# Gated attention and FFN mix on one core: the second FFN product summed in three blocks a token tile instead of one

## The chip, the cores and the metric

The kernel runs on 1 core of one Trainium2 chip. The metric is device time in microseconds; three runs of the kernel before took 1418.3, 1418.87 and 1421.13 us, median 1418.87 us. All other numbers of the time before come from one execution that was profiled.

## What is computed

Two branches over the same 2048 tokens of width 512, mixed by a gate for each token. Branch A is softmax attention with 32 heads of 16; branch B is a gated FFN of width 1792. Everything is fp32; the kernel splits each fp32 operand of its dense products into a high and a low part and adds three products (high by high, high by low, low by high).

```python
x = A_x
g = sigmoid((x * gate_w).sum(-1, keepdims=True))
a = softmax(q @ k.T * 16 ** -0.5) @ v @ wo      # per head; q, k, v = x @ wqkv
b = (silu(x @ w1) * (x @ w3)) @ w2
out = g * a + (1 - g) * b
```

## The kernel before

After a preparation of some 95 us the program is one long list of TensorE work that is written out by hand. The string `order` (lines 734 to 738) has a letter for each piece of TensorE work, and the loop at line 743 walks it:

- Q: one unit of scores, 128 keys by 512 queries for two heads (`score`, line 713). Its two matmuls go to two halves of the array's rows and of a two-bank PSUM tile `S`, of which there are two. ScalarE takes the exponential of the unit (line 723) into a tile `p`.
- P: two units of `p` times V, into the bank `acc` (`pv`, line 702). With the last key tile, `evac` (line 685) copies `acc` out and sends it to DRAM.
- F: one step of the dense work, by `feed` (line 654).

A period of the first 83 (`one`) is 8 Q, 21 F and 4 P; a later one (`two`) is 8 Q, 15 F and 4 P. The last one has 6 Q, 12 F and 4 P. In all there are 2418 F in the string; what is left of the dense work then runs alone, in the loop at line 779. After it come, at full height of the array, the products of the output projection that need the last head (lines 784 to 820). They wait for a chain of transfers that begins with the last `evac`: row sums out to DRAM and back, a reciprocal, out and back again, a multiplication, a split into halves (lines 773 and 776 to 816).

A step F gives one matmul to each of two lanes: rows 0 to 63 of the array (upper) and rows 64 to 127 (lower). A block is one PSUM bank of output. The upper lane runs all its products of a block over the first 64 contraction rows, then the lower lane runs the same number over the other 64 rows into the same bank, while the upper lane is at the next block. Three rules of `feed` set the pace:

```python
used = st["started"] - 3
if st["upper"] is None and (used < 0 or used < st["ended"] and left_at[used] + rest <= clock):
...
if st["lower"] is None and ready and ready[0][0] + gap <= issued:
```

There are three banks, so the upper lane starts a block only if the block three earlier has ended, and 7 counts have gone by since (`rest`; Q and F are one count, P is four). The lower lane takes a block when 3 scores have been issued since the upper lane left it (`gap`). If a lane has nothing, the step holds one matmul, or none.

The blocks, in order (`blocks`, line 630): 136 of 12 products a lane (q and k projections, then the FFN's first half, line 409), 16 of 42 products (the FFN's second half, one for each tile of 128 tokens, `h_product`, line 514), and 6 of 12 (the output projection of token tiles 0 to 5, `o_product`, line 592). The 42 are 14 row tiles of w2 by three products. VectorE takes each finished bank out of PSUM: for the second half, `h_done` (line 529) multiplies it by 1 - g into a tile `gs` and sends that to the DRAM tensor `B_d`, from where it comes back for the final sum in `mix` (line 601).

When the lower lane has done a quarter of a tile's products, line 520 loads and splits the same quarter for the tile after next (`load_piece`, `halves_of`): a transfer by SP's queue into a staging tile `sg`, then two GpSimd operations. The loads of the next head pair's Q and K (`load_step`, line 269), the stores of `evac` and the fetches of `divide` (line 564) go through the same SP queue, in program order. The reciprocal of `divide` (line 555) stands in VectorE's order among the evictions and waits for a transfer.

Of the kernel before, what the change touches and what calls it, by code (L numbers as in the profile page):

```python
# [8 lines left out]
F32 = mybir.dt.float32  # L9
# [3 lines left out]
OP = mybir.AluOpType  # L13
# [11 lines left out]
NT = S // P  # L25
ND = D // P
NF = F // P
# [6 lines left out]
def gated_mix_kernel(ctx: ExitStack, tc: tile.TileContext, x, wqkv, wo, w1, w3, w2, gate_w, out):  # L34
# [18 lines left out]
    nc = tc.nc  # L53
# [27 lines left out]
    def slot(tag, dtype=F32R, shape=(P, 512)):  # L81

        return (fw if tag[0] == "f" else fk).tile(list(shape), dtype, name=tag, bufs=BUFS.get(tag, 2))
# [4 lines left out]
    def bank():  # L88
        return psum.tile([P, 512], F32, name="f", bufs=3)
# [13 lines left out]
    omg = const.tile([P, NT], F32, name="omg")  # L103
# [206 lines left out]
    def load_weights(chunk):  # L310
        out = []
        for n, w in zip("13", chunk["src"]):
            r = slot("fr", F32, (P, ND, P))
            nc.sync.dma_start(r, w.rearrange("(k p) n -> p k n", p=P))
            if chunk["first"]:
                wh = slot("raw", F32R, (P, ND, P))
                wl = slot("raw" if n == "1" else "gw", F32R, (P, ND, P))
            else:
                wh = slot("fh" + n, F32R, (P, ND, P))
                wl = slot("fl" + n, F32R, (P, ND, P))  # L320
            nc.gpsimd.tensor_copy(wh, r)  # L321
            nc.gpsimd.tensor_sub(wl, r, wh)
            out.append((wh, wl))
        chunk["w"] = out

    chunks = [dict(src=(wqkv[:, P * c:P * c + P], wqkv[:, D + P * c:D + P * c + P]), first=c == 1)
              for c in range(1, ND)]
# [77 lines left out]
    def w_product(chunk, which, b):  # L405
        def product(ps, r, n):
            w = chunk["w"][which]
            k, i = divmod(n, 3)
            nc.tensor.matmul(ps, w[i == 2][r, k, :], (xL if i == 1 else xH)[b][r, k, :],  # L409
                             start=n == 0 and r.start == 0, stop=n == 3 * ND - 1 and r.start > 0)  # L410
        return product
# [3 lines left out]
    def qk_done(c, i, b):  # L415
        def done(ps):
            nonlocal qk_left
            lo = slot("gs", F32)
            hi = slot("sg")
            nc.vector.tensor_copy(lo, ps)  # L420
            nc.gpsimd.tensor_copy(hi, lo)
            nc.gpsimd.tensor_sub(lo, lo, hi)
            store_qk(i, c, b, hi, lo)
            qk_left -= 1
        return done
# [71 lines left out]
    def load_piece(t, q):  # L497
        hi, lo = (slot(SETS[t % 2][2 * q + i]) for i in range(2))
        tag = "fr" if t == 0 or t == 1 and q < 2 else "sg"
        n = min(4, NF - 4 * q)  # L500
        src = h_d[512 * q:512 * q + P * n, P * t:P * t + P].rearrange("(f p) t -> p f t", p=P)
        halves_of(src, hi[:, 0:P * n], lo[:, 0:P * n], tag)
        hs.setdefault(t, []).append((hi, lo))

    def load_wo(k):
        if k < 2:
            hi, lo = w2H[3][:, 2 + k, :], w2L[3][:, 2 + k, :]
        else:
            both = wk.tile([P, 2, 512], F32R, name=f"p{NP - k + 1}")
            hi, lo = both[:, 0, :], both[:, 1, :]  # L510
        halves_of(wo[P * k:P * k + P, :], hi, lo, "sg")
        wo_[k] = hi, lo

    def h_product(t):
        def product(ps, r, n):
            f, i = divmod(n, 3)
            q, o = divmod(f, 4)
            nc.tensor.matmul(ps, hs[t][q][i == 2][r, P * o:P * o + P], (w2L if i == 1 else w2H)[q][r, o, :],  # L518
                             start=n == 0 and r.start == 0, stop=n == 3 * NF - 1 and r.start > 0)
            if r.start and i == 2 and (o == 3 or f == NF - 1):  # L520
                if t + 2 < NT:
                    load_piece(t + 2, q)
                elif t == NT - 2:
                    load_ot(q)
                elif q < 2:
                    load_ot(4 + q)
        return product

    def h_done(t):
        def done(ps):  # L530
            y = slot("gs", F32)
            nc.vector.tensor_scalar(y, ps, omg[:, t:t + 1], None, op0=OP.mult)  # L532
            nc.sync.dma_start(B_d[P * t:P * t + P, :], y)
            if t in (4, 5, 6):
                later.append(lambda: load_wo((0, 1, 3)[t - 4]))
            if t == NT - 1:
                stages.append(rest_of_o())
        return done


    def load_ot(t):
        n = (0, 1, 2, 3, 2, 3, 0, 1)[t]
        hi, lo = (slot(SETS[0][2 * n + i]) for i in range(2))
        halves_of(N_d[:, P * t:P * t + P].rearrange("(k p) t -> p k t", p=P), hi[:], lo[:], "fr" if t >= 4 else "sg")
        ot[t] = hi, lo
# [46 lines left out]
    def o_product(t):  # L592
        def product(ps, r, n):
            if n == 0 and r.start:
                load_bt(t)
            k, i = divmod(n, 3)
            nc.tensor.matmul(ps, ot[t][i == 2][r, P * k:P * k + P], wo_[k][i == 1][r, :],  # L597
                             start=n == 0 and r.start == 0, stop=n == 3 * ND - 1 and r.start > 0)
        return product
# [5 lines left out]
    def o_done(t):  # L605
        def done(ps):
            mix(t, ps)
            if t < 2:
                load_ot(t + 6)
            if t in (3, 4):  # L610
                load_bt(t + 3, "fh1" if t == 3 else "fh3")
        return done
# [10 lines left out]
    def rest_of_o():  # L623
        for k in range(ND - 1):
            for b in (2, 3):
                load_o(k, b)
                for _ in range(4):
                    yield

    def blocks():  # L630
        last = len(chunks) - 1
        turns = [(m, b) for m in range(last - 1) for b in range(NB)]
        turns += [(last - i, b) for two in ((0, 1), (2,), (3,)) for i in (1, 0) for b in two]
        for m, b in turns:
            for which in range(2):
                if m < ND - 1:
                    yield w_product(chunks[m], which, b), qk_done(m + 1, which, b), 3 * ND
                else:
                    yield w_product(chunks[m], which, b), (up_done if which else gate_done)(m - ND + 1, b), 3 * ND
                if (b, which) == (1, 0) and m < last - 1 or (m, b, which) == (last - 1, 0, 1):  # L640
                    load_weights(chunks[m + 1])
        for t in range(NT):
            yield h_product(t), h_done(t), 3 * NF
        for t in range(NT // 2 - 2):
            yield o_product(t), o_done(t), 3 * ND

    NBLOCK = 8 * len(chunks) + NT + NT // 2 - 2
    source = blocks()

    ready, state_f = [], dict(upper=None, lower=None, started=0, ended=0)  # L650
# [128 lines left out]
    while feed(0, 0):  # L779
        pass  # L780
    assert state_f["ended"] == NBLOCK and not small and not later and not stages and not soon and not loads


    for t in (NT // 2 - 2, NT // 2 - 1):
        ps = bank()
# [4 lines left out]
    for t in range(NT // 2, NT):  # L790
        n, r = divmod(t - NT // 2, 2)
# [6 lines left out]
        if r == 0:  # L798
            y = wk.tile([P, 2, 512], F32, name=f"p{free.pop(0)}")
# [12 lines left out]
    for b in (2, 3):  # L812
        o, r = orr[b - 2]
# [34 lines left out]
```

## Time and profile before

| what | number |
|---|---|
| median of three runs | 1418.87 us (1418.3 to 1421.13) |
| profiled execution | span 1417.6 us, 1.3 us under that median; the page gives no time of it beside the span |
| TensorE matmul, busy | 1408.8 us, 99% |
| ScalarE, busy | 1033.2 us, 73%, of which the exponentials 967.5 us |
| VectorE, busy | 449.4 us, 32% |
| GpSimd, busy | 321.1 us, 23% |

Rows of a timeline read: start in us, duration in us, engine, line, operation, output and inputs by the program's names, shapes, and how many alike were merged (x). A bracket gives the idle time of the engine before it and what ended it. Rows of a group give total busy time and the mean in ns of one. A matmul's duration is longer than its distance to the next one, since matmuls are pipelined: the pace is read from the starts. PEld is the loading of weights, which overlaps the matmuls, SPq the issuing of transfers by SP's queue.

### The profile page before, as it was taken

How to read it: one execution, taken by the hardware profiler on the slowest of the kernel's cores; microseconds unless marked ns; L12 is line 12 of the kernel's file. 1: busy time of each engine (PE TensorE's matmuls, PEld its weight loads, DVE VectorE, ACT ScalarE, POOL GpSimd, SP SyncE). 2: the span in 40 equal slices, each digit the busy share in tenths (PEclk: the TensorE clock that was granted, in tenths of full speed). 3: DMA queues.
4: the chain of work that ended last, by engine and by line, in shares of the span. 5: the costliest groups of instructions: out<-in, count | busy, mean ns of one | idle time of the engine just before them, and what ended most of it. 6: DMA issues, size and time to landing. Idle time of an engine off the chain costs nothing.

```text
span 1417.6 us, 28518 instructions
## 1 busy us (share of the span) xinstructions
PE 1408.8 (99%) x11399; PEld 833.7 (59%) x11399; DVE 449.4 (32%) x845; ACT 1033.2 (73%) x1153; POOL 321.1 (23%) x356
## 2 busy tenths in 40 slices
PE   9999999999999999999999999999999999999998
PEld 7865656656556566565565665655555555554556
DVE  4421102464555545455464545400000000000013
ACT  4556767777777777777777777777788778877870
POOL 5014443011011100110110015441332332233230
PEclk9999999999999999999999999999999999999999
DMA  7554455342124432223233234543534443345445
GB/s 197 141 121 114 126 140 128 73 110 69 46 61 85 113 69 61 70 72 87 68 76 79 76 81 122 136 101 74 126 81 102 104 105 70 66 112 106 106 133 182
DMA packets 112668, 141.42 MB, mean 100 GB/s; under 512 B 16400, under 2 KB 70672, under 8 KB 109456
## 3 DMA queue, kind: packets, MB, share of 16 engines
q1 hardware_dynamic: 110384, 135.72, 39.6%
q10 hardware_dynamic: 2144, 3.80, 0.8%
q8 instruction: 92, 1.51, 0.5%
q14 instruction: 48, 0.39, 0.1%
HBM read 90.70 MB, written 48.76 MB: 98 GB/s over the span
## 4 chain that ended last, share of the span: by engine, by line
PE 93%; POOL 0%; DMA 0%; DVE 0%; ACT 0%; issue 0%; SPq 0%; ACTq 0%; POOLq 0%
PE acc L706 32%; PE f L409 27%; PE S L719 19%; PE f L518 11%; PE f L597 1%; PE f L95 0%; PE f L97 0%; PE f L96 0%; DMA fr<-in_B_w_dram 0%; PE S L97 0%; PE S L96 0%; PE S L95 0%; POOL xL L489 0%; POOL fl L489 0%; DVE sg L458 0%; POOL xH L488 0%
## 5 line engine op out<-in xcount | busy, mean ns | idle before, releaser
L723 ACT ACTIVATE p<-S 128x1024 f32<-128x1024 f32 x1024 | 967.5, 1026 | 308.4 <-PE S L719 307.1
L706 PE MATMUL acc<-p,V 128*17 128x512 f32 x4096 | 473.5, 594 | 0.0
L719 PE MATMUL S<-Qt,Kt 50*128 50x512 f32 x2048 | 427.9, 413 | 1.1 <-POOLq L278 0.6
L719 PEld LDWEIGHTS S<-Qt,Kt 50*128 50x128 f32 x2048 | 193.8, 184 | 187.4 <-ACT p L723 80.4
L706 PEld LDWEIGHTS acc<-p,V 128*17 128x17 f32 x4096 | 102.8, 97 | 274.1 <-issue 273.9
L409 PE MATMUL f<-xL,fh 64*128 64x512 f32 x1024 | 205.1, 391 | 0.0
L409 PE MATMUL f<-xH,fl 64*128 64x512 f32 x1024 | 204.9, 390 | 0.0
L409 PE MATMUL f<-xH,fh 64*128 64x512 f32 x1024 | 204.7, 390 | 0.0
L440 DVE RECIPROCAL sg<-sg 128x64 f32<-128x64 f32 x448 | 201.2, 509 | 1.9
L409 PEld LDWEIGHTS f<-xL,fh 64*128 64x128 f32 x1024 | 99.4, 187 | 21.2
L409 PEld LDWEIGHTS f<-xH,fl 64*128 64x128 f32 x1024 | 98.5, 185 | 20.1
L409 PEld LDWEIGHTS f<-xH,fh 64*128 64x128 f32 x1024 | 99.4, 187 | 17.7
L321 POOL CAST fh<-fr 128x512 fp32r<-128x512 f32 x32 | 21.6, 674 | 371.1 <-DMA fr<-in_B_w_dram 246.5
L687 DVE COPY u<-acc 128x512 f32<-128x512 f32 x32 | 22.1, 692 | 257.0 <-PE acc L706 257.0
L518 PE MATMUL f<-xH,fl 64*128 64x512 f32 x224 | 82.2, 391 | 0.5 <-POOL fl L489 0.5
L518 PE MATMUL f<-xL,fh 64*128 64x512 f32 x224 | 82.2, 391 | 0.3 <-POOL xL L489 0.3
L518 PE MATMUL f<-xH,fh 64*128 64x512 f32 x224 | 82.1, 391 | 0.0
L518 PE MATMUL f<-xH,raw 64*128 64x512 f32 x192 | 74.9, 390 | 0.0
L532 DVE TENSOR_SCALAR gs<-f,omg 128x512 f32<-128x512 f32 x16 | 12.0, 751 | 176.4 <-PE f L518 176.4
L432 DVE COPY gs<-f 128x512 f32<-128x512 f32 x56 | 38.7, 691 | 78.1 <-PE f L409 78.1
L518 PE MATMUL f<-xH,fr 64*128 64x512 f32 x160 | 62.4, 390 | 0.0
L454 DVE TENSOR_TENSOR raw<-f,gs 128x512 f32<-128x512 f32 x50 | 34.1, 682 | 82.7 <-PE f L409 82.7
(216 smaller groups left out, 1309.6 us busy)
## 6 DMA issues: line engine op xcount, KB each, us to landing
Kt<-kH_d SPq DMA_DIRECT2D x128, 128.0 KB
h_d<-sg SPq DMA_DIRECT2D x56, 256.0 KB
sg<-h_d SPq DMA_DIRECT2D x43, 256.0 KB
fr<-in_B_w_dram SPq DMA_DIRECT2D x42, 256.0 KB
Qt<-qH_d SPq DMA_DIRECT2D x128, 64.0 KB
Kt<-kL_d SPq DMA_DIRECT2D x64, 128.0 KB
fr<-in_A_wqkv_dram SPq DMA_DIRECT2D x18, 256.0 KB
Qt<-qL_d SPq DMA_DIRECT2D x64, 64.0 KB
```

Of the source, the lines that this page charges most:

```text
L321: nc.gpsimd.tensor_copy(wh, r)
L409: nc.tensor.matmul(ps, w[i == 2][r, k, :], (xL if i == 1 else xH)[b][r, k, :], start=n == 0 and r.start == 0, stop=n == 3 * ND - 1 and r.s ...
L432: nc.vector.tensor_copy(gs, ps)
L440: small.append(lambda q=q: nc.vector.reciprocal(sg[:, q:q + 64], sg[:, q:q + 64]))
L454: nc.vector.tensor_mul(gu, ps, st["gs"])
L518: nc.tensor.matmul(ps, hs[t][q][i == 2][r, P * o:P * o + P], (w2L if i == 1 else w2H)[q][r, o, :], start=n == 0 and r.start == 0, stop=n = ...
L532: nc.vector.tensor_scalar(y, ps, omg[:, t:t + 1], None, op0=OP.mult)
L597: nc.tensor.matmul(ps, ot[t][i == 2][r, P * k:P * k + P], wo_[k][i == 1][r, :], start=n == 0 and r.start == 0, stop=n == 3 * ND - 1 and r. ...
L687: nc.vector.tensor_copy(u, acc)
L706: nc.tensor.matmul(acc[r:r + DH + 1, :], V[:, k, 2 * j + h, :], p[:, h, :], start=k == 0, stop=k == NT - 1)
L719: nc.tensor.matmul(ps[:, h, :], Kt[i][r:r + 50, P * k:P * k + P], Qt[i][r:r + 50, t:t + 512], start=True, stop=True)
L723: nc.scalar.activation(p, ps, AF.Exp, scale=SCALE)
```

## The change

Each token tile of the second FFN half becomes three blocks of 14 products a lane. The first block's eviction multiplies by 1 - g into `gs`, as before; the second and third take the bank times 1 - g plus `gs` in one VectorE operation (`scalar_tensor_tensor`), and the third sends the result off. The products, their order and their operands are the same; a block boundary can fall inside the three products of one row tile of w2. The transfers and splits of the pieces hang on the same products as before.

```diff
+    PART = NF
+    y_ = {}
+
-    def h_product(t):
+    def h_product(t, part):
         def product(ps, r, n):
-            f, i = divmod(n, 3)
+            f, i = divmod(PART * part + n, 3)
             q, o = divmod(f, 4)
             nc.tensor.matmul(ps, hs[t][q][i == 2][r, P * o:P * o + P], (w2L if i == 1 else w2H)[q][r, o, :],
-                             start=n == 0 and r.start == 0, stop=n == 3 * NF - 1 and r.start > 0)
+                             start=n == 0 and r.start == 0, stop=n == PART - 1 and r.start > 0)
...
-    def h_done(t):
+    def h_done(t, part):
         def done(ps):
-            y = slot("gs", F32)
-            nc.vector.tensor_scalar(y, ps, omg[:, t:t + 1], None, op0=OP.mult)
+            if part == 0:
+                y_[t] = slot("gs", F32)
+                nc.vector.tensor_scalar(y_[t], ps, omg[:, t:t + 1], None, op0=OP.mult)
+                return
+            y = y_[t]
+            nc.vector.scalar_tensor_tensor(y, ps, omg[:, t:t + 1], y, op0=OP.mult, op1=OP.add)
+            if part == 1:
+                return
             nc.sync.dma_start(B_d[P * t:P * t + P, :], y)
...
         for t in range(NT):
-            yield h_product(t), h_done(t), 3 * NF
+            for part in range(3):
+                yield h_product(t, part), h_done(t, part), PART
...
-    NBLOCK = 8 * len(chunks) + NT + NT // 2 - 2
+    NBLOCK = 8 * len(chunks) + 3 * NT + NT // 2 - 2
```

## The prediction

> **What bounds the kernel now.** I read the page first, then TensorE's waits, then the busy time in the stage that the change touches (about 900 us to the last score at 1382), and then the order of instructions in its last 60 us.
>
> ```profile
> PE 1408.8 (99%) x11399; PEld 833.7 (59%) x11399; DVE 449.4 (32%) x845; ACT 1033.2 (73%) x1153; POOL 321.1 (23%) x356
> PE 93%; POOL 0%; DMA 0%; DVE 0%; ACT 0%; issue 0%; SPq 0%; ACTq 0%; POOLq 0%
> ```
>
> ```profile
> PE f L518 <- POOL fl L489: 0.5, 1, 0.5
> ```
>
> ```profile
> 929.00:1348.00 419.00, 419.00 (x3446) 222.09 (x3446) 21.79 (x31) 334.64 (x353) 123.72 (x141) 1.00 0.43 97
> ```
>
> The first two rows say that the chain that ends last is TensorE's own work, 93% of it. The third is one of only two waits of the FFN's second half (L518) for another engine, 0.5 us. The fourth is nearly the whole of that second half: TensorE is busy 419 of 419 us at full clock (1.00), VectorE 21.79 us. So only fewer TensorE steps can make the kernel shorter; more VectorE work alone costs nothing there.
>
> **What a step costs.** First a stretch with both lanes at work, then one with a single lane:
>
> ```profile
> 508.13 0.40 PE L719 MATMUL S<-Qt,Kt 50*128 50x512 f32 x2
> 508.37 0.40 PE L409 MATMUL f<-xH,fh 64*128 64x512 f32 x2
> 508.59 0.40 PE L409 MATMUL f<-xL,fh 64*128 64x512 f32 x2
> 508.83 0.40 PE L409 MATMUL f<-xH,fl 64*128 64x512 f32 x2
> 509.06 0.40 PE L719 MATMUL S<-Qt,Kt 50*128 50x512 f32 x2
> ```
>
> ```profile
> 1331.26 0.40 PE L719 MATMUL S<-Qt,Kt 50*128 50x512 f32 x1
> 1331.50 0.39 PE L518 MATMUL f<-xH,fr 64*128 64x512 f32 x1
> 1331.73 0.39 PE L518 MATMUL f<-xL,fr 64*128 64x512 f32 x1
> 1331.90 0.50 PE L719 MATMUL S<-Qt,Kt 50*128 50x512 f32 x1
> 1331.96 0.39 PE L518 MATMUL f<-xH,fr 64*128 64x512 f32 x1
> 1332.19 0.39 PE L719 MATMUL S<-Qt,Kt 50*128 50x512 f32 x1
> ```
>
> A score and three steps take 509.06 - 508.13 = 0.93 us with pairs (x2) and 1332.19 - 1331.26 = 0.93 us with single matmuls (x1). A step costs 0.23 us whether it carries one matmul or two. Half-filled steps are the waste that shorter blocks can remove.
>
> **How many steps go.** The work is fixed: 136 x 12 + 16 x 42 + 6 x 12 = 2376 products a lane, 4752 in two lanes. Steps that carry anything = (4752 + single steps) / 2. I walked the order string by feed's rules. Before, single steps are 18 at the start, 30 where the long blocks begin (the lower lane has finished a block of 12 and waits until the upper lane is through 42), and 48 where they end (the lower lane alone finishes 42 while the upper lane, out of banks after a block or two, stands still; then the last blocks): 96, so 2424 steps, the string's 2418 and 6 after it. After, 18, 3, 4 and 19: 44, so 2398 steps. The last 20 F of the string stay empty and nothing is left over. So 26 steps go, 26 x 0.23 = 6.0 us if each is worth its pace. But the order is fixed and all steps up to the 2398th are still filled: until about 1370 us nothing can come sooner. The 26 lie at the very end, and must be priced there.
>
> **The 20 empty F of the last periods.** There ScalarE is beside TensorE:
>
> ```profile
> 1366.79 5.66 ACT L723 ACTIVATE p<-S 128x1024 f32<-128x1024 f32 x6 [0.56 <-PE S L719]
> 1376.20 4.74 ACT L723 ACTIVATE p<-S 128x1024 f32<-128x1024 f32 x5 [0.56 <-PE S L719]
> ```
>
> ```profile
> 1370.65 0.50 PE L719 MATMUL S<-Qt,Kt 50*128 50x512 f32 x1
> 1370.69 0.39 PE L597 MATMUL f<-xH,fl 64*128 64x512 f32 x1
> 1370.93 0.40 PE L719 MATMUL S<-Qt,Kt 50*128 50x512 f32 x1
> ```
>
> ```profile
> 1379.14 0.50 PE L719 MATMUL S<-Qt,Kt 50*128 50x512 f32 x1
> 1379.20 0.39 PE L597 MATMUL f<-xH,fl 64*128 64x512 f32 x1
> 1379.43 0.39 PE L719 MATMUL S<-Qt,Kt 50*128 50x512 f32 x1
> 1379.74 1.91 PE L706 MATMUL acc<-p,V 128*17 128x512 f32 x16
> ```
>
> Inside each run of scores the exponentials follow each other without a gap; a run of six takes 5.66 us, one of five 4.74, so one more costs 0.92 us. That is the pace of a score with three steps. Two S tiles exist, so a score waits for the exponential two before it: with the F gone, ScalarE holds the same pace. What is gained is the last score of each run. Half of it goes at 1379.14, the other half stands behind the F of 1379.20 until 1379.43; without that F the whole of it goes at 1379.14, and the P behind it (1379.74) starts 0.29 us sooner. The run before gives 1370.93 - 1370.65 = 0.28 us in the same way, and the gap of 0.56 us ahead of 1376.20 shows that ScalarE was idle there, so the 0.28 is passed on. Together 0.5 us (bounds: 0, if ScalarE gives nothing, and 20 x 0.23 = 4.6, if it could go at any pace; I take the rows' own 0.5, since the gapless runs speak against the upper end).
>
> **The 6 steps after the string.**
>
> ```profile
> 1384.24 0.72 PE L597 MATMUL f<-p,fh 64*128 64x512 f32 x2
> 1384.80 0.39 PE L597 MATMUL f<-p,fl 64*128 64x512 f32 x1
> ...
> 1385.50 0.39 PE L597 MATMUL f<-p,fl 64*128 64x512 f32 x1
> 1385.83 0.51 PE L95 MATMUL f<-xH,raw 128*128 128x512 f32 x1
> ```
>
> L95 takes the place of the first of them: 1385.83 - 1384.24 = 1.59 us, or 6 x 0.23 = 1.4 us if the change from half to full rows keeps its extra 0.1 us. I take 1.5. It counts only if the end is still TensorE's and not that of the chain of transfers behind the last eviction:
>
> ```profile
> 1404.94 0.69 DVE L816 TENSOR_TENSOR p<-fr,p 128x512 fp32r<-128x512 f32 x1 [0.70 <-ACT p L815]
> 1407.62 0.39 PE L97 MATMUL acc<-p,xL 128*128 128x512 f32 x1
> 1407.85 0.39 PE L95 MATMUL S<-p,p 128*128 128x512 f32 x1
> ```
>
> That chain's last operand is ready at 1404.94 + 0.69 = 1405.63; TensorE, at the filling work until 1407.85, comes to it 2.2 us later. With 1.5 us less filling 0.7 us of cover is left; without any cover the gain here would be 0.
>
> **The added evictions: 32 VectorE operations.** Their form, one PSUM input, a scalar column and a second tile, stands in the trace as L602, beside the one that they add to:
>
> ```profile
> L532 DVE TENSOR_SCALAR gs<-f,omg 128x512 f32<-128x512 f32 x16 | 12.0, 751 | 176.4 <-PE f L518 176.4
> L602 DVE SCALAR_TENSOR_TENSOR gs<-f,g,gs 128x512 f32<-128x512 f32 x6 | 4.4, 734 | 26.7 <-PE f L597 14.3 <-DMA fr<-n_d 6.4 <-DMA gs<-b_d 6.1
> ```
>
> 32 x 0.74 = 24 us on an engine that has 21.79 of 419 us. Hidden, as long as the bank is free when the upper lane wants it:
>
> ```profile
> 944.64 0.39 PE L518 MATMUL f<-xH,fl 64*128 64x512 f32 x1
> 945.09 0.75 DVE L532 TENSOR_SCALAR gs<-f,omg 128x512 f32<-128x512 f32 x1 [15.54 <-PE f L518]
> ```
>
> From the last matmul's start to the end of the eviction: 945.84 - 944.64 = 1.20 us. By feed's rules the tightest hand-over of the changed order has 8 counts (3 of 48; 12 have 9), 8 x 0.23 = 1.85 us. It fits with 0.6 us to spare. A waiting instruction ahead of an eviction would eat that. The only one is the reciprocal of `divide`:
>
> ```profile
> 987.67 0.55 DVE L555 RECIPROCAL dd<-dd 128x64 f32<-128x64 f32 x1 [16.09 <-DMA dd<-d_d]
> 989.15 0.39 PE L518 MATMUL f<-xL,fh 64*128 64x512 f32 x1
> ```
>
> It ends at 988.22. The first 14-step block that ends behind it in program order ends with the step at 989.15, its eviction is due at 989.6. In the changed order this transfer also stands ahead of a piece's load in SP's queue, not behind it. Cost 0; the bound above is a stall at the hand-overs (rival 2), and nothing here can bring a gain.
>
> The rule of the Trainium skill that speaks against the change is in "TensorEngine Tiling (Array Packing)", section "PSUM Bottleneck": tiling quickens TensorE but not the emptying of PSUM, and the copy may become the bound. By the rows above the copy takes 1.20 us of 1.85, so the sum stays; by the rule it would be the second rival's.
>
> **What is moved.** No transfer is added. The pieces of the tile after next are issued sooner, since the lower lane follows the upper lane by some 20 steps, not 47; the first ones now stand ahead of the next step's Q and K loads on SP:
>
> ```profile
> 933.00 0.45 SPq L261 DMA_DIRECT2D Qt<-qH_d  x1
> 938.59 0.58 SPq L266 DMA_DIRECT2D Qt<-m_d  x2
> ```
>
> ```profile
> 969.73 0.69 DVE L687 COPY u<-acc 128x512 f32<-128x512 f32 x1 [23.89 <-PE acc L706]
> ```
>
> These loads are issued by 939.2 and first used when the next step begins, about 969: 30 us of cover for a few us of delay. Cost 0; the upper lane's own pieces come no later.
>
> **The sum**, against the span of 1417.6: - 0.5 - 1.5 + 0 = - 2.0, so 1415.6. The median of the runs lies 1.3 above the span, which gives 1416.9, -0.14%.
>
> **Rivals.**
> 1. Every step is worth its pace: the exponentials close up where the F are gone. Then -6.0: 1418.9 - 6.0 = 1412.9. For it: ScalarE is busy only 73%. Against: the gapless runs at 0.92 us. Something between also falls here.
> 2. Slower: the bank hand-over. Three times as many blocks each wait for their eviction. It decides from the point where an eviction ends later than 1.85 us after the last matmul's start (now 1.20). Priced by the one wait on record in this stage, 0.5 us, on the 15 tightest hand-overs: +7.5, less the 2.0 gained, 1418.9 + 5.5 = 1424.4; with half of that wait, 1420.6. For it: for blocks of 42 the hand-over has 84 counts or more, for blocks of 14 as few as 8. Against: 0.6 us of room, an almost idle engine.
> 3. The end is the transfers' already: the cover of 2.2 us is used up, by a slower round trip, and the 1.5 us are lost. -0.5, 1418.4.
>
> **How the numbers follow.** Forecast 0.66, rival 1 0.12, rival 2 0.12, rival 3 0.10. About 0.2% (2.8 us) is what a measurement of this kernel tells from no change. The forecast lies 0.8 us inside that line; with runs that differ by 2.8 us among themselves I give 0.10 of its 0.66 to faster and 0.01 to slower. Faster 0.10 + 0.12 = 0.22, same 0.55 + 0.10 = 0.65, slower 0.13. The range takes in the bound of the last score runs, halfway (-2.0 - 2.3, 1414.6, and 0.8 for the spread of the runs: 1413.8), and above rival 3 and the mild end of rival 2, 1420.0.
>
> **What would show it.** In the profile after: L518 without single steps at its beginning; TensorE's waits without VectorE; the same start of scores up to about 1365; then runs of exponentials still 0.92 us apart; no L597 behind the last P, and L95 at once. Wrong would be: TensorE waiting for the evictions of L518, exponentials closer than 0.9 us, or a gap before the last L95 to L97.

## The result and the profile after

| kernel | median | lowest to highest | runs |
|---|---|---|---|
| before | 1419.28 us | 1418.3 to 1423.97 | 6 |
| changed | 1429.76 us | 1426.31 to 1432.16 | 6 |

The ratio is 1.0065, with a 95% interval from 1.0047 to 1.0083: slower, where about no change was forecast (1416.9 us, 1413.8 to 1420.0). Runs of every kernel here, before too, fall for the most part in two groups some 4 to 5 us apart, of which the slower has a low TensorE clock at 85 to 98 us, ahead of anything that the change touches, so kernels are compared within a group where less than that matters (last section).

The profiled execution of the changed kernel took 1432.06 us, span 1430.2, against a span of 1417.6 before: 12.6 us more. From its page, the busy times and the chain that ended last:

```profile
PE 1413.1 (99%) x11399; PEld 833.5 (58%) x11399; DVE 473.2 (33%) x877; ACT 1034.0 (72%) x1153; POOL 321.0 (22%) x356
PE 91%; SPq 1%; DMA 1%; ACT 0%; POOL 0%; issue 0%; DVE 0%; ACTq 0%; DVEq 0%; POOLq 0%
```

The number of matmuls is the same, VectorE has the 32 operations more (877 - 845) and 23.8 us more work. The new thing is in the second row: SP's queue and DMA have 1% each of the chain; both had 0% before.

**Where the 12.6 us lie.** The copies of `acc` at the end of each step of the scores are milestones that both kernels have. The last three, first in the timeline of before, then of after (L697 is the old L687):

```profile
1309.66 0.69 DVE L687 COPY u<-acc 128x512 f32<-128x512 f32 x1 [23.64 <-PE acc L706]
1347.35 0.69 DVE L687 COPY u<-acc 128x512 f32<-128x512 f32 x1 [6.63 <-PE acc L706]
1384.35 0.69 DVE L687 COPY u<-acc 128x512 f32<-128x512 f32 x1 [5.83 <-PE acc L706]
```

```profile
1314.28 0.69 DVE L697 COPY u<-acc 128x512 f32<-128x512 f32 x1 [4.79 <-PE acc L716]
1360.35 0.69 DVE L697 COPY u<-acc 128x512 f32<-128x512 f32 x1 [7.09 <-PE acc L716]
1398.59 0.69 DVE L697 COPY u<-acc 128x512 f32<-128x512 f32 x1 [16.04 <-PE acc L716]
```

| stretch | before | after | difference |
|---|---|---|---|
| start to the first of the three | 1309.66 | 1314.28 | +4.62 |
| to the second | 37.69 | 46.07 | +8.38 |
| to the third (the last scores) | 37.00 | 38.24 | +1.24 |
| to the end of the span | 33.25 | 31.61 | -1.64 |

The four differences sum to 12.60. The first is the early low clock, not the change's: at the first copy of all (129.43 before, 134.44 after) the distance is 5.01 us already, and from 929 to 1310 us, with the new blocks at work, it stays between 4.59 and 4.63. The change's own are the other three: +8.0 us together, which is also the distance of the 1426.31 to 1427.57 of after from the 1418.3 to 1419.41 of before.

**The +8.38.** TensorE's waits in after, the two longest:

```profile
PE f L606 <- DVE gs L611: 5.5, 1, 5.5
PE S L729 <- ACT p L733: 3.1, 6, 0.9
```

The first row is new: one wait of 5.5 us of an output-projection block (L606, formerly L597) for a bank, which `mix` (L611) has not taken out. In time, TensorE and VectorE around it, from the timeline of after:

```profile
1336.81 0.40 PE L729 MATMUL S<-Qt,Kt 50*128 50x512 f32 x2
1342.73 0.76 PE L606 MATMUL f<-xH,fh 64*128 64x512 f32 x1 [5.52 <-DVE gs L611]
1344.73 3.61 PE L716 MATMUL acc<-p,V 128*17 128x512 f32 x16
```

```profile
1327.15 0.75 DVE L539 SCALAR_TENSOR_TENSOR gs<-f,omg,gs 128x512 f32<-128x512 f32 x1 [8.46 <-PE f L521]
1341.83 0.75 DVE L611 SCALAR_TENSOR_TENSOR gs<-f,g,gs 128x512 f32<-128x512 f32 x1 [13.92 <-DMA gs<-b_d]
```

VectorE was idle for 13.92 us before that `mix`; the bracket names the load of `gs` from `B_d`. So the engine is not the bottleneck, its input is late. SP's queue says why. First its wait of before, then that of after, then its timeline at that place in before, then in after:

```profile
SPq L487 <- PE f L518: 10.9, 1, 10.9
```

```profile
SPq L487 <- PE S L729: 17.7, 1, 17.7
```

```profile
1321.61 0.57 SPq L266 DMA_DIRECT2D Qt<-m_d  x2
1333.07 1.18 SPq L487 DMA_DIRECT2D fr<-n_d  x2
```

```profile
1306.80 0.46 SPq L542 DMA_DIRECT2D b_d<-gs  x1
1324.82 0.36 SPq L487 DMA_DIRECT2D fr<-n_d  x1
1325.23 1.24 SPq L703 DMA_DIRECT2D d_d<-u  x4
...
1328.72 0.50 SPq L261 DMA_DIRECT2D Qt<-qH_d  x1
...
1336.13 0.35 SPq L542 DMA_DIRECT2D b_d<-gs  x1
1336.53 0.42 SPq L599 DMA_DIRECT2D gs<-b_d  x1
```

From 1307.3 to 1324.8 the queue issues nothing. It stands at the load of output-projection tile 4 (`load_ot`), which wants the staging tile `fr`. The three `fr` buffers also hold pieces of h for the third and fourth quarters of the last FFN tile, and `product` issues this load when that tile's first quarter has passed the lower lane, in both kernels. With shorter blocks the lower lane passes it sooner: against the first of the three copies, SP reaches the load 12.5 us after it before (1322.2) and 7.0 us ahead of it in after (1307.3), but the buffer comes free only 10.5 us behind the copy. Everything behind the load waits too: the stores of the copy of 1314.28 (issued at 1325.23), the next step's Q and K, the last store to `B_d` (its block was out at 1327.90, the store goes at 1336.13), and the first load from `B_d` (1336.53), which lands just before the `mix` of 1341.83. Before, the same wait existed (10.9 us, 1322.2 to 1333.07), but it lay between two copies; the next step's Q and K had been issued by 1322.2, and no load from `B_d` was due.

The wait of TensorE makes 5.7 of the 8.38 us: from the start of the matmul before to the start of the one that waited are 1342.73 - 1336.81 = 5.92 us, where the pace is 0.23 (the 5.52 of the row count from the end of the matmul before). The rest is the clock. From the windows of after (PE, PEld, DVE, ACT, POOL busy, then the granted clock, the DMA share and GB/s):

```profile
929.00:1348.00 419.00, 413.48 (x3406) 217.60 (x3402) 45.11 (x62) 327.03 (x345) 129.56 (x149) 0.99 0.43 100
1343.00:1352.00 9.00, 9.00 (x54) 3.15 (x55) 0.00 (x0) 3.58 (x4) 8.60 (x10) 0.71 0.45 147
1386.00:1392.00 6.00, 4.22 (x30) 1.32 (x30) 0.00 (x0) 4.93 (x6) 0.00 (x0) 1.00 0.01 3
1392.00:1398.00 6.00, 6.00 (x36) 1.36 (x36) 0.00 (x0) 2.72 (x3) 0.00 (x0) 0.72 0.00 0
```

After the wait TensorE gets 0.71 of its clock for 9 us, which takes 9 x 0.29 = 2.6 us from it, and a group of 16 products P takes 3.61 us instead of 1.91: 5.7 + 2.6 = 8.3. In the first row VectorE's busy time has doubled (21.79 to 45.11 us) while TensorE's recorded idle time is that of the one wait alone, 419.00 - 413.48 = 5.52: no eviction of the new blocks holds TensorE up there.

**The +1.24.** TensorE and ScalarE in the last run of scores, in after:

```profile
1390.08 0.49 PE L729 MATMUL S<-Qt,Kt 50*128 50x512 f32 x2 [0.94 <-ACT p L733]
...
1392.35 3.35 PE L716 MATMUL acc<-p,V 128*17 128x512 f32 x16
1396.26 2.29 PE L716 MATMUL acc<-p,V 128*17 128x512 f32 x16
1398.47 0.50 PE L95 MATMUL f<-xH,raw 128*128 128x512 f32 x1
```

```profile
1389.01 4.69 ACT L733 ACTIVATE p<-S 128x1024 f32<-128x1024 f32 x5 [0.57 <-PE S L729]
```

Five exponentials take 4.69 us (4.74 before): ScalarE sets the pace, as forecast. TensorE now stands idle for ScalarE six times, 3.1 us in all and 0.94 at most, and right behind, from 1392 on, it is granted 0.72 of its clock (the last row of the windows): the groups P, which nothing paces but TensorE, take 3.35 and 2.29 us instead of 1.91. The filling work of L95 follows the last P at once, so the -1.64 of the table is there.

### The profile page after: what moved, and what is told of

Its sections match the earlier page's. It is cut to its first block, busy times and chain, and to the rows that moved or that the text cites. A ratio compares the mean times of both kernels' runs of the same rounds, so it can differ in the third digit from the quotient of the medians.

```text
span 1430.2 us, 28598 instructions
## 1 busy us (share of the span) xinstructions
PE 1413.1 (99%) x11399; PEld 833.5 (58%) x11399; DVE 473.2 (33%) x877; ACT 1034.0 (72%) x1153; POOL 321.0 (22%) x356
## 4 chain that ended last, share of the span: by engine, by line
PE 91%; SPq 1%; DMA 1%; ACT 0%; POOL 0%; issue 0%; DVE 0%; ACTq 0%; DVEq 0%; POOLq 0%
PE acc L716 32%; PE f L409 27%; PE S L729 19%; PE f L521 10%; PE f L606 1%; ACT p L733 0%; DMA gs<-b_d 0%; PE f L95 0%; PE f L96 0%; PE f L97 0%; DMA fr<-in_B_w_dram 0%; PE S L96 0%; PE S L95 0%; PE S L97 0%; SPq L261 0%
## 5 line engine op out<-in xcount | busy, mean ns | idle before, releaser
L409 PE MATMUL f<-xL,fh 64*128 64x512 f32 x1024 | 205.2, 391 | 0.0
L409 PE MATMUL f<-xH,fh 64*128 64x512 f32 x1024 | 204.8, 390 | 0.0
L409 PEld LDWEIGHTS f<-xH,fh 64*128 64x128 f32 x1024 | 99.5, 187 | 17.7
L539 DVE SCALAR_TENSOR_TENSOR gs<-f,omg,gs 128x512 f32<-128x512 f32 x32 | 23.9, 748 | 196.0 <-PE f L521 196.0
L521 PE MATMUL f<-xL,fh 64*128 64x512 f32 x224 | 75.7, 391 | 0.0
L521 PE MATMUL f<-xH,fh 64*128 64x512 f32 x224 | 75.6, 391 | 0.0
L521 PE MATMUL f<-xH,raw 64*128 64x512 f32 x192 | 70.0, 391 | 0.0
L697 DVE COPY u<-acc 128x512 f32<-128x512 f32 x32 | 22.1, 692 | 144.5 <-PE acc L716 144.5
L438 DVE TENSOR_SCALAR sg<-sg 128x512 f32<-128x512 f32 x56 | 26.8, 478 | 102.1 <-ACT sg L437 99.1
```

The source lines that it names most:

```text
L438: small.append(lambda: nc.vector.tensor_scalar(sg, sg, 1.0, None, op0=OP.add))
L539: nc.vector.scalar_tensor_tensor(y, ps, omg[:, t:t + 1], y, op0=OP.mult, op1=OP.add)
L697: nc.vector.tensor_copy(u, acc)
```

## The experiments

Two causes are claimed so far, SP's wait for `fr` and the clock in the emptied steps; a third, the bank hand-overs, is denied. The first four kernels go for the two causes, the next two for the third, the last two for what is left to win. Each line number of an experiment is its own.

**1. The loads of the output projection staged in `sg`, in the changed kernel.** The load no longer needs the tile that it waited for.

```diff
-        halves_of(..., hi[:], lo[:], "fr" if t >= 4 else "sg")
+        halves_of(..., hi[:], lo[:], "sg")
```

> The changed kernel with one tag altered: the halves for token tiles 4 to 7 of the output projection are staged in sg, not in fr. Theory 1 (SP's queue stands still because the load for tile 4 waits for an fr buffer that holds the last token tile's h pieces, and the eviction's stores, the next Q and K loads, the last B_d store and the first B_d load queue up behind it): SP's longest wait for TensorE at a piece load falls from 17.7 us to under 5, the 5.5 us wait of TensorE for the mix disappears, no low clock around 1337 to 1352; 8.4 us less than the changed kernel, so within 2 us of the kernel before (ratio 0.998 to 1.001), if the low clock at 85 to 98 us is absent or shared. Theory 2 (the evictions of shorter blocks hold the banks): nothing changes, ratio 1.005 to 1.008. TensorE's low clock in the emptied steps (0.72 near 1392 in the changed kernel) should remain under both.

Measured: 1423.03 us median of 12 (1419.31 to 1424.84), ratio to before 1.0011 [0.9996, 1.0025]. Its four runs with the highest mean clock (1419.31 to 1420.0) stand against 1418.91 us, the median of those runs of before; its five with the lowest (1424.26 to 1424.84) against 1423.61: about +1.0 in each group. Three lie between the groups. Its last copies and its `mix`, from its timeline:

```profile
1308.87 0.69 DVE L697 COPY u<-acc 128x512 f32<-128x512 f32 x1 [4.78 <-PE acc L716]
...
1330.21 0.75 DVE L611 SCALAR_TENSOR_TENSOR gs<-f,g,gs 128x512 f32<-128x512 f32 x1 [7.72 <-PE f L606]
...
1346.58 0.69 DVE L697 COPY u<-acc 128x512 f32<-128x512 f32 x1 [7.10 <-PE acc L716]
...
1386.35 0.69 DVE L697 COPY u<-acc 128x512 f32<-128x512 f32 x1 [17.55 <-PE acc L716]
```

`mix` now waits for TensorE's block, not for a DMA, and the stretch that had +8.38 is 37.71 us, +0.02. The stretch of the last scores is 39.77 us, +2.77 over before: the clock drops more here (granted 0.61 from 1370 to 1374 us, and again behind it: its last P groups begin with 3.48 us). So the staging tile accounts for the whole of the 8.38, and the emptied steps still cost.

**2. The same loads in `fr`, but issued two quarters later, in the changed kernel.** Another way to the same end: the tile stays, the time moves.

```diff
-                elif q < 2:
-                    load_ot(4 + q)
+                elif q >= 2:
+                    load_ot(2 + q)
```

> The changed kernel, with fr kept, but the loads for tiles 4 and 5 are issued when the last token tile's third and fourth quarter are done, not the first and second. Theory 1 says that the wait in SP's queue is the cause and not the staging tile as such: no wait over 5 us of SP's piece loads for TensorE, no 5.5 us wait of TensorE, time as e1 within 1 us. Rival: the loads themselves or their bandwidth late in the kernel cost the time; then as the changed kernel, ratio about 1.006.

Measured: 1421.63 us median of 10 (1417.95 to 1424.58), ratio 1.0009 [0.9996, 1.0023]. Its wait in SP's queue and its last two copies:

```profile
SPq L487 <- PE S L729: 0.7, 1, 0.7
```

```profile
1347.13 0.69 DVE L697 COPY u<-acc 128x512 f32<-128x512 f32 x1 [7.10 <-PE acc L716]
...
1385.44 0.69 DVE L697 COPY u<-acc 128x512 f32<-128x512 f32 x1 [16.09 <-PE acc L716]
```

17.7 us of queue wait became 0.7, the loss of 8.38 is gone (the copy before these two is at 1309.42, 37.71 us ahead of the first), and the last stretch is 38.31 us, +1.31, as in after. At the highest clock its runs take 1417.95 to 1418.91 us, 1.0 below the four of experiment 1 by their medians; in the last stretch experiment 1 loses 39.77 - 38.31 = 1.46 us more. Two edits that share only the removed wait have the same effect: that the wait of the queue was the cause is shown.

**3. The staging in `sg`, in the kernel before.** If the edit were worth something by itself, it would show here.

> The kernel before with the same tag altered as in e1. There SP's wait for the fr buffer (10.9 us) falls between two evictions with nothing urgent behind it. Theory 1: SP's wait goes, the time stays within 0.7 us of before (ratio 0.9995 to 1.0005). If it gains 2 us or more, the wait already cost time before the change.

Measured: 1423.1 us median of 10 (1418.42 to 1424.61), ratio 1.0007 [0.9992, 1.0021]; at the highest clock 1418.42 to 1418.5, against 1418.91. The wait of 10.9 us is gone from the queue and the time stays within 0.5 us: before, it was harmless, as its place between two copies said. The queue now stands 17.2 us at the next store to `B_d` instead, whose block isn't done, and that costs nothing either: not the length of a queue's wait counts, but what is due behind it.

**4. Experiment 1, with the empty steps filled.** An F that finds no work issues one matmul, 20 in all, into a spare bank; nobody reads its result.

```diff
+    spare = []
+    def fill():
+        if not spare:
+            spare.append(bank())
+        nc.tensor.matmul(spare[0], wo_[0][0][0:64, 0:P], wo_[0][0][0:64, :], start=True, stop=True)
...
         elif c == "F":
-            feed()
+            if not feed():
+                fill()
```

> As e1, and each of the 20 empty F of the string carries one matmul of 64 rows into a spare bank that nobody reads (work added, 20 matmuls). Theory 3 (the emptied steps leave TensorE idle for 0.4 to 0.9 us at a time, the granted clock falls to 0.72, and the last P group takes 3.35 us in place of 1.91): with the fill the clock stays 1.00 and the last P groups take 1.9 us; 1 to 1.5 us faster than e1, 1.5 to 2 us faster than before (ratio 0.9985 to 0.999). Rival (the slow P group waits for exponentials, not for the clock): no gain over e1, or up to 1 us lost by the added work.

Measured: 1418.01 us median of 12 (1416.52 to 1422.59), ratio 0.9985 [0.997, 0.9999]; by groups 1417.2 against 1418.91, and 1422.1 against 1423.61, so 1.5 to 1.7 us faster than before and some 2.6 faster than experiment 1 (1 to 1.5 were expected; experiment 1 had lost 2.77 in the last stretch, not 1.24). Its windows and its timeline in the last scores:

```profile
1380.00:1386.00 6.00, 6.00 (x41) 3.26 (x43) 0.00 (x0) 4.75 (x6) 0.00 (x0) 1.00 0.00 0
```

```profile
1351.16 0.69 DVE L704 COPY u<-acc 128x512 f32<-128x512 f32 x1 [7.10 <-PE acc L723]
...
1388.00 0.69 DVE L704 COPY u<-acc 128x512 f32<-128x512 f32 x1 [14.63 <-PE acc L723]
```

The clock stays at 1.00, the stretch is 36.84 us, 0.16 under before. More TensorE work made the kernel shorter. That the emptied steps cost by the clock is shown. What they would bring at full clock is not: with the fillers each step takes its 0.23 us again.

**5 and 6. Evictions doubled and tripled, on top of experiment 4.** Each of the 48 evictions of the second half is followed by one or two further operations on the same bank and tile (the first block's is done over again, the others add 0 times the bank). The doubled one:

```diff
-                nc.vector.tensor_scalar(y_[t], ps, omg[:, t:t + 1], None, op0=OP.mult)
+                for _ in range(2):
+                    nc.vector.tensor_scalar(y_[t], ps, omg[:, t:t + 1], None, op0=OP.mult)
...
             nc.vector.scalar_tensor_tensor(y, ps, omg[:, t:t + 1], y, op0=OP.mult, op1=OP.add)
+            nc.vector.scalar_tensor_tensor(y, ps, 0.0, y, op0=OP.mult, op1=OP.add)
```

> As e4, with each eviction of the FFN's second half made of two VectorE operations (the second adds zero times the bank). By the prediction's sum an eviction then ends 1.20 + 0.73 = 1.93 us after the last matmul's start, 0.08 us behind the tightest 3 hand-overs (1.85 us) and before all others: up to 0.5 us slower than e4. Rival (each hand-over costs TensorE something, whatever its margin): 48 hand-overs, 3 us or more over e4.

> As e8 with three operations: an eviction ends 2.66 us after the last matmul's start. By the hand-overs of the order (3 of 8 counts, 12 of 9, 7 of 10, 7 of 11, at 0.23 us a count) TensorE waits 0.81, 0.58, 0.35 and 0.12 us there: 13 us in all, some of it given back where the exponentials lag. So 8 to 14 us slower than e4, with waits of TensorE for VectorE at L521's line in the waits. If the time stays, the hand-over's margin was misjudged.

Measured: doubled 1418.63 us median of 10 (1418.21 to 1423.48), by groups 1418.56 and 1423.04: +1.4 and +0.9 over experiment 4, where at most 0.5 was expected. Tripled 1434.41 us median of 4 (1432.38 to 1436.85), +15.2 and +14.5. The waits of TensorE for evictions, doubled, with TensorE and VectorE at that place:

```profile
PE f L521 <- DVE gs L541: 1.0, 1, 1.0
```

```profile
1108.72 0.55 DVE L566 RECIPROCAL dd<-dd 128x64 f32<-128x64 f32 x1 [8.42 <-DMA dd<-d_d]
1109.19 0.65 DVE L540 SCALAR_TENSOR_TENSOR gs<-f,omg,gs 128x512 f32<-128x512 f32 x1
1109.87 0.69 DVE L541 SCALAR_TENSOR_TENSOR gs<-f,gs 128x512 f32<-128x512 f32 x1
...
1110.71 0.47 PE L521 MATMUL f<-xH,gw 64*128 64x512 f32 x1 [0.97 <-DVE gs L541]
```

And tripled:

```profile
PE f L521 <- DVE gs L542: 6.3, 14, 0.5
PE f L521 <- DVE gs L537: 2.2, 7, 0.4
```

One more operation of 0.69 us moves the end of an eviction from 1.20 to 1.89 us behind the last matmul's start. Only one wait of TensorE for an eviction is recorded, and it lies where the reciprocal of `divide` stands right ahead of the eviction. Two more operations move the end to 2.6 us, and 21 hand-overs wait, 8.5 us by the record.

The order string, walked by feed's rules, shows a slip in the prediction's count: the three hand-overs of 8 counts are not among the 48 of the second half. They are those at which the output projection's blocks 3 to 5 take a bank that `mix` empties, and the wait of 5.5 us in after is at the first of them. The tightest of the 48 are the 12 with 9 counts, 9 x 0.23 = 2.07 us. So 1.89 still fits and 2.6 doesn't: between the two lies the point from which the hand-over decides, as the prediction's rival had it, and the change was on the safe side. Of the 15 us of the tripled evictions the waits on record hold 8.5. A recorded wait begins at the end of the matmul before, 0.39 us after its start, where the pace is 0.23, so some 21 x 0.16 = 3.4 us more are an estimate for what the record leaves out; the other 3 us stay open.

**7. One tile more of the output projection in the string, on top of experiment 4.** Token tile 6 becomes a block of 12 products, so that 12 of the 20 empty F have work, and 12 full-height products fall away at the end.

```diff
-            if t in (3, 4):
-                load_bt(t + 3, "fh1" if t == 3 else "fh3")
+            if t == 4:
+                load_bt(t + 3, "fh3")
...
-        for t in range(NT // 2 - 2):
+        for t in range(NT // 2 - 1):
...
-    for t in (NT // 2 - 2, NT // 2 - 1):
+    for t in (NT // 2 - 1,):
```

> As e4, but token tile 6 of the output projection goes through the lanes as a seventh block of 12, so that 12 of the 20 empty F carry its products, 8 carry the fill, and 12 full-height matmuls fewer stand behind the last P. Theory (the 20 steps are free room beside the exponentials as long as TensorE's clock holds): 12 x 0.23 = 2.8 us faster than e4, 4 to 5 us faster than before (ratio 0.9965 to 0.998), with a cover of 4.2 us less 1.6 less 2.8 ahead of the last head's operands left near 0. Rival: the chain of transfers behind the last eviction takes over, a gap of 0.5 us or more stands ahead of the last products and the gain is under 2 us.

Measured: 1417.45 us median of 12 (1414.42 to 1421.69) against 1419.1 for before on the same chip, ratio 0.9975 [0.996, 0.9991]; by groups 1416.2 against 1418.93 and 1420.42 against 1423.45, 2.7 and 3.0 us faster, where 4 to 5 were expected. That is about 0.2%. From its last copy at 1388.24 to its end at 1418.6 are 30.36 us, where experiment 4 takes 1419.7 - 1388.00 = 31.70: 1.34 us came of the 12 x 0.23 = 2.8 us removed. ScalarE and TensorE at the place:

```profile
1406.65 0.63 ACT L833 ACTIVATE p<-fr 128x512 fp32r<-128x512 f32 x1 [19.56 <-DVE fr L832]
1408.65 0.63 ACT L833 ACTIVATE p<-fr 128x512 fp32r<-128x512 f32 x1 [1.36 <-DVE fr L832]
```

```profile
1407.34 0.50 PE L95 MATMUL S<-p,p 128*128 128x512 f32 x1
...
1409.33 0.50 PE L95 MATMUL f<-p,p 128*128 128x512 f32 x1
```

The first operand is ready at 1407.28 and TensorE takes it at 1407.34: 19.10 us behind the last copy, against 1409.91 - 1388.00 = 21.91 in experiment 4, so the full 2.8 us came this far. From there TensorE follows its operands one by one (the next of ScalarE is ready at 1409.28, taken at 1409.33): its 24 last products take 6.26 us from the first start to the last (1413.60), against 5.21 (1409.91 to 1415.12), and from the last start to the end of the span are 5.00 us against 4.58. The cover of the transfers' chain is used up: the rival had this, though as one gap of 0.5 us or more, which no row shows.

**8. Two tiles more**, the same edit with all eight tiles in the string and none behind it.

> As e6, with token tile 7 too: no F is empty, 4 single steps are left over behind the string, and 24 full-height matmuls fewer stand behind the last P than in e4 (5.5 us less, 0.9 us more). By the cover of 4.2 us the chain of transfers decides now: TensorE waits 0.5 to 2.5 us ahead of the last products, time within 1 us of e6. If nothing waits, 1.8 us faster than e6.

Measured: 1420.2 us median of 12 (1415.4 to 1421.72), ratio 0.9988 [0.9973, 1.0003]; by groups within 0.3 us of experiment 7. A row of its waits that no other kernel has:

```profile
PE S L95 <- ACT p L831: 0.9, 1, 0.9
```

TensorE waits for the operand of the last heads: from here on the round trip of the row sums sets the end, and less TensorE work brought nothing.

## Why the prediction was wrong

- **"What is moved ... Cost 0": this step failed, and it is the 8.4 us.** It asked what the pieces that are issued sooner are moved ahead of, and weighed a few us of delay against 30 us of cover. It did not ask what each moved load itself waits for. The pieces of the second half wait for nothing scarce, but line 520 also issues the output projection's loads, and the one of tile 4 came some 20 us sooner against the scores to a staging tile that came free only 13 us sooner. The wait (10.9 us) stands in the profile of before, among SP's waits. The loss shows as a bank that VectorE has not emptied, rival 2's kind of wait, but not for rival 2's reason: the eviction that was late is `mix` of the output projection, ahead of which VectorE stood idle for 13.92 us until its load had landed. "The only one is the reciprocal of `divide`", said of instructions that wait ahead of an eviction, was wrong too: `mix` itself waits for a load, as the prediction's own row L602 has it (6.1 us of idle time, `<-DMA gs<-b_d`).
- **"The 20 empty F of the last periods", -0.5: the clock was put at nothing.** The reading of ScalarE was right: the exponentials stay 0.92 to 0.94 us apart. Rival 1 (each step worth its pace) falls with it. What came of it is +1.24, outside the bounds of 0 to 4.6 us gained: a TensorE that waits up to 0.94 us at a time loses its clock, and 6 us at 0.72 cost 6 x 0.28 = 1.7 us. The difference, 1.24 - 1.7, is about -0.4, near the forecast's -0.5; that is an estimate, and no run shows the empty steps at full clock. With the steps filled (experiment 4) the stretch is 0.16 us under before.
- **"The 6 steps after the string", -1.5:** measured -1.64 in after and 33.25 - 31.70 = -1.55 in experiment 4. The cover of the transfers' chain held; rival 3 did not come, but experiments 7 and 8 meet that chain.
- **"The added evictions", 0:** right, with the rate too:

```profile
L539 DVE SCALAR_TENSOR_TENSOR gs<-f,omg,gs 128x512 f32<-128x512 f32 x32 | 23.9, 748 | 196.0 <-PE f L521 196.0
```

  748 ns for each of the 32 (0.74 forecast), and no TensorE wait for them. Experiments 5 and 6 enclose rival 2's point of decision. A part of it was luck: the prediction looked at one reciprocal of `divide` (987.67), and three stand in that stage. The second (1108.63 in after) does hold an eviction up: its block's last matmul starts at 1107.95, so it was due 0.45 us later, at 1108.40, and began at 1109.10. It ends at 1109.75, and TensorE takes the bank at 1110.04: room was left, but not by the prediction's sum.
- **The count of steps** (26 fewer, 20 empty) holds: experiment 4 has 20 matmuls more (11419 for 11399), one for each empty F. With the two losses repaired the forecast's sum, -2.0, stands beside a measured -1.5 to -1.7.

## What to carry to other kernels

When a change makes work end earlier, list every transfer whose issue hangs on that work and ask for each which buffer it needs and when that buffer's last reader is through; in an in-order queue the price is paid by whatever is behind it, here a load that had nothing to do with the change. A queue's wait that is harmless before is a warning, not a proof. And steps that are removed beside another engine's pace were not free to remove here: fillers that kept TensorE busy brought 2.6 us, and useful work in their place (experiment 7) more.

## What the runs showed of the hardware that was not expected

**Short gaps lower the clock.** In after no gap of the last scores is longer than 0.94 us, TensorE is busy 4.22 of 6 us, and the grant falls to 0.72 over the next 6 us; with 20 fillers it stays at 1.00. The Trainium skill, "TensorE: Matmul & The Clock Gate", Part 1, has the clock fall after an idle window of some 3.4 us. For the wait of 5.52 us, with 0.71 behind it, the trace agrees; for the last scores that rule alone does not give the fall, since no gap there comes near 3.4 us.

**A low clock early in the run, in some runs only.** The windows from 85 to 98 us, in the profiled execution of before and then of after:

```profile
85.00:98.00 13.00, 12.16 (x84) 7.22 (x86) 0.45 (x1) 9.27 (x10) 0.18 (x1) 1.00 0.54 96
```

```profile
85.00:98.00 13.00, 11.84 (x48) 8.91 (x49) 0.32 (x1) 8.19 (x9) 0.00 (x0) 0.65 0.54 95
```

It isn't the change's: of 35 runs of before beside experiments 1 to 4, 17 had a mean clock of 0.999 or more and took 1418.38 to 1419.82 us (median 1418.91), and 18 had 0.994 to 0.996 and took 1422.64 to 1425.96 (median 1423.61). TensorE's busy time doesn't tell the two apart: 12.16 and 11.84 of 13 us here, and 12.49 at a grant of 0.61 in the profiled run of experiment 4. What decides it was not tried.
